# Quarter 3's down-projections as pairs of 128x64 matrices, with a new written-out instruction order

## The chip, the cores and the metric

One core of a Trainium2 chip runs the whole program. The metric is the time of one execution on the device, in microseconds (us), as the median of several runs; lower is better. Engines are named as in the profile: PE is TensorE (PEld its weight loads), DVE is VectorE, ACT is ScalarE, POOL is GpSimd, SP is the queue that issues most DMAs.

## What is computed

```python
def _A_ref(q, k, v, shift_k, ssm_k, ssm_D):      # B=1, S=2048, D=512
    # k_shift[t] = sum over 4 taps of k[t - j] * shift_k[:, j]
    kv = k_shift * v
    # y = causal long convolution of kv with ssm_k along S, by FFTs of length 2S
    y = y + kv * ssm_D[None, None, :]
    return q * y

def _B_ref(x, w_gate, w_up, w_down):             # 512 -> 1792 -> 512
    h = _gelu(x @ w_gate) * (x @ w_up)
    return h @ w_down

x = A_q
xn = _layernorm(x, axis=-1)
s = _A_ref(xn, A_k, A_v, A_shift_k, A_ssm_k, A_ssm_D)
g = _silu(_B_ref(xn, B_w_gate, B_w_up, B_w_down))
return x + s * g
```

All inputs are bf16.

## The kernel before

The 2048 rows are cut into four quarters of 512. The feed-forward part does, for each quarter `q` (0 to 3), fourteen units: a unit is one 128-column block of the gate and of the up projection, four matmuls of 128x128 weights against 512 columns of the transposed normalised input `xnT` for each of the two. ACT takes the gelu of the gate out of PSUM (`GE`, line 1194), DVE multiplies it with the up product (`HT`, line 1203), which also gives the PSUM bank back. `down(q)` then multiplies `HT` with `Wd`: per 128-row tile `jt` fourteen 128x128 matmuls of 512 columns that add up in one PSUM bank, in three tasks of 4, 5 and 5. For the last tile of quarter 3 the columns are split 384 + 128, so that the very last piece is short. `xnT` of quarters 0 and 1 is made on PE; that of quarters 2 and 3 by one DMA transpose each (line 884), issued from SP, in a single buffer per quarter parity. The normalisation of a tile (`XN`, lines 870 on ACT and 871 on DVE) may be placed on either engine.

The convolution part is a staged transform. Its PE work is in smaller matrices: halves of 64x128 (lines 950 and 959), 32x32 matrices, sixteen side by side (line 1028, for `BH`, `BK` and the inverse `MI`), and, as its last stage (line 1270, called y below), eight pieces j of two pairs each: two 128x64 matrices side by side, one writing PSUM partitions 0 to 63, the other 64 to 127, at `tile_position=(0, 0)` and `(0, 64)`. Between the stages the data passes through DRAM scratch (`ZH`, `ZK`, `ZI`) and comes back transposed by DMA into `BH`, `BK`, `BI`. The 32x32 stage on `BH` is evicted to `HSW` by ACT or DVE, a swap of its rows by two DMAs (`HSW<-HSW`) makes a second copy, and DVE multiplies these with the evicted `KB` (line 1131).

For y, a piece is copied out of PSUM (`BO`, line 633 on ACT or 636 on DVE) and multiplied by DVE into `G` or `XN` (line 1287), for tiles 0 to 11 with the residual added (line 1299) and sent out. For quarter 3, ACT takes the Silu of the down-projection (line 1235), and DVE multiplies and adds (lines 1237 and 1238) before the output DMA.

The order is written out by hand-off: `SEQ` is a list of 816 task numbers (a `b` behind a number takes the task's second engine, DVE in place of ACT or the reverse), found by a search; every engine gets its instructions in that order, and semaphores hold each until its inputs are there. At most four PSUM banks (`NF_BANKS = 4`) belong to units and down-projections at a time. `SEQ`, the costs and due times beside it say what the search assumed; at run time only the order counts.

Of the kernel before, what the change touches and what calls it, by code (L numbers as in the profile page):

```python
# [7 lines left out]
FP32 = mybir.dt.float32  # L8
# [10 lines left out]
MF = FF // 128  # L19
NQ = 4  # L20
# [4 lines left out]
N_WARM = 12  # L25
ORDER = "x00 h0 x01 w0 D0 h1 w1 h2 h3 s0 k0 w2 x1 k1 k2 w3 d0 d1 v0 v1 k3 v2 v3 x2 x3"
SEQ = (
# [23 lines left out]
)  # L51
NF_BANKS = 4
ISSUE = 470.0
# [361 lines left out]
def build_kernel(nc, A_q, A_k, A_v, A_shift_k, A_ssm_k, A_ssm_D, B_w_gate, B_w_up, B_w_down, out):  # L415
    with ExitStack() as es0:
# [11 lines left out]
        def new(name, shape, dt):  # L428
            h = at(name, shape, dt, place["at"])
            place["at"] += size(shape, dt)  # L430
            return h
# [3 lines left out]
        Wd = new("Wd", [128, MF, DM], BF16)  # L435
# [10 lines left out]
        ident = new("ident", [128, 128], BF16)  # L446
        ident32 = new("ident32", [128, 128], FP32)
        COLS = new("COLS", [128, 8], FP32)
        stats = new("stats", [128, NT, 6], FP32)
        mv = new("mv", [128, NT, 4], FP32)  # L450
        NHALF = new("NHALF", [128, 4, 1], FP32)
        EPSC = new("EPSC", [128, 1, 1], FP32)
        NB_ = new("NB_", [128, NT, 1], FP32)
        SKB = new("SKB", [128, 4, DM], BF16)
        skb_at = place["at"] - 4 * DM * 2
# [9 lines left out]
        HT = new("HT", [128, 2, MF, 512], BF16)  # L465
# [51 lines left out]
        trk = Trk(nc, block)  # L517
# [15 lines left out]
        def R_bank(b):  # L533
            return [R_ps[b.slot // 2][b.slot % 2]]
# [19 lines left out]
        R_HT = [[res(f"HT{j}_{m}", HT[:, j, m, :]) for m in range(MF)] for j in range(2)]  # L554
# [86 lines left out]
        def mm(h, o, l, r, st, sp):  # L641
            return h.matmul(o, lhsT=l, rhs=r, start=st, stop=sp)  # L642
# [145 lines left out]
        R_Wd = [res(f"Wd{i}", Wd[:, 7 * i:7 * i + 7, :]) for i in range(2)]  # L788
# [137 lines left out]
        for k in range(KD):  # L926
# [4 lines left out]
                    r=[bHD, *[bHTr[k][0] for k in range(KD)]], w=[bFold], rr=[R_D, *R_HTr[0]], ww=R_HTr[0])  # L931
# [274 lines left out]
        def down(q):  # L1206
            for jt in range(4):
                t = 4 * q + jt
                cols = [(0, DM)] if t < NT - 1 else [(0, 384), (384, DM)]
                for c0, c1 in cols:  # L1210
                    p = B(f"psd{q}_{jt}_{c0}", pF)

                    def pc(p=p, c0=c0, c1=c1):
                        return bank(p)[:, c0:c1]

                    for m0, m1 in ((0, 4), (4, 9), (9, 14)):
                        def f(e, p=p, jt=jt, m0=m0, m1=m1, pc=pc, c0=c0, c1=c1):
                            for m in range(m0, m1):
                                trk.op("PE", lambda h, m=m: mm(h, pc(), HT[:, q % 2, m, 128 * jt:128 * (jt + 1)], Wd[:, m, c0:c1], m == 0, m == MF - 1),
                                       r=[R_HT[q % 2][m], R_Wd[m // 7]], w=R_bank(p), accum=True)  # L1220
                        down_tasks[q].append(S.add([("PE", pe(m1 - m0, c1 - c0))], f, r=(bHT[q] if jt else bHT[q][m0:m1]) + bWd[m0 // 7:(m1 + 6) // 7],
                                                   w=[p], lat=150.0))
                    n = c1 - c0
                    g, rg = G[:, t, c0:c1], [R_G[t] if n == DM else R_Gh[c0 > 0]]
                    bt = B(f"tanh{q}_{jt}")
                    if q < NQ - 1:
# [3 lines left out]
                           r=[p, bt], w=[bG[t // 2]], rr=lambda p=p, rg=rg: R_bank(p) + rg, ww=rg)  # L1230
# [11 lines left out]
                          r=[b2], w=[B(f"outl{t}")], nbytes=256 * n)  # L1242
# [14 lines left out]
        for j in range(8):  # L1257
            p, bi = p_y[j], b_bi[j]
# [98 lines left out]
```

## Time and profile before

| | |
|---|---|
| median of 3 runs | 190.72 us (190.45 to 190.84) |
| span of the profiled execution (first to last instruction) | 189.2 us |
| granted TensorE clock, mean | 0.997 |
| PE busy | 182.8 us, 1406 matmuls recorded |
| DVE busy | 165.5 us, 250 instructions |
| ACT busy | 141.6 us, 196 instructions |

The profile has no time of its own for that execution beside its span: the 1.5 us between 189.2 and 190.72 lie around the span (start and end of the program). Busy time of PE overlaps from one matmul to the next: a matmul's row lasts about 0.38 us though one starts every 0.216 us, so the distance between starts is what counts. Some matmul records are missing, 1406 of 1418; where one is missing the profile shows 0.16 us of "issue" on PE or a row with one matmul fewer.

### The profile page before, as it was taken

The numbers are of one execution on the slowest core, as the hardware profiler recorded it, in microseconds if no ns is written. First come the engines' busy times: TensorE is split into PE (matmuls) and PEld (weight loads), VectorE is DVE, ScalarE is ACT, GpSimd is POOL, SyncE is SP. The second block draws the span as 40 slices with busy tenths as digits, with TensorE's granted clock in tenths as the row PEclk, the third lists the DMA queues.
The fourth block names the chain that finished last, engine by engine and source line by source line (L and its number), as shares of the span: only waits on it lengthen the run. The fifth ranks groups of instructions, "written<-read, shape, count | busy, mean of one in ns | idle before, by whom it ended". The sixth has DMA issues, their size and how long they took to land.

```text
span 189.2 us, 3591 instructions
## 1 busy us (share of the span) xinstructions
PE 182.8 (97%) x1406; PEld 80.6 (43%) x1418; DVE 165.5 (87%) x250; ACT 141.6 (75%) x196; POOL 10.4 (5%) x26
## 2 busy tenths in 40 slices
PE   7899999999999999999999999999999999999992
PEld 2685544544333334334444443433333344444441
DVE  6889999999999999978589599999999964658695
ACT  3749797998879798799638897998999575323971
POOL 5312302000000000022000000000000000000000
PEclk9999999999999999999999999999999999999998
DMA  5999999999584996557999997499345254908754
GB/s 177 319 381 297 366 380 360 402 415 297 166 309 150 335 287 229 166 187 235 301 310 173 333 322 251 144 299 326 135 162 170 97 181 146 376 36 283 268 186 153
DMA packets 36422, 47.84 MB, mean 253 GB/s; under 512 B 7347, under 2 KB 26039, under 8 KB 36406
## 3 DMA queue, kind: packets, MB, share of 16 engines
q1 hardware_dynamic: 29878, 39.23, 63.6%
q10 hardware_dynamic: 6528, 8.39, 12.8%
q8 instruction: 11, 0.18, 0.4%
q14 instruction: 5, 0.04, 0.1%
HBM read 27.39 MB, written 14.68 MB: 222 GB/s over the span
## 4 chain that ended last, share of the span: by engine, by line
PE 79%; DVE 15%; ACT 3%; issue 2%
PE psall L642 67%; PE psall L1028 6%; DVE KTM L1009 3%; DVE KAC L1011 2%; PE psall L916 2%; PE psall L950 2%; DVE HT L1203 1%; DVE G L1299 1%; PE psall L959 1%; PE psall L1270 1%; DVE G L1287 1%; DVE XN L965 1%; DVE G L1238 1%; DVE G L1237 1%; ACT XN L870 1%
## 5 line engine op out<-in xcount | busy, mean ns | idle before, releaser
L642 PE MATMUL psall<-xnT,Wu 128*128 128x512 bf16 (+1 forms) x248 | 56.0, 359 | 0.0
L642 PE MATMUL psall<-xnT,Wg 128*128 128x512 bf16 (+1 forms) x248 | 55.3, 359 | 0.5 <-DVE xnT L636 0.5
L642 PE MATMUL psall<-Wd,HT 128*128 128x512 bf16 (+2 forms) x226 | 50.3, 366 | 1.2 <-issue 0.8
L1194 ACT ACTIVATE GE<-psall 128x512 bf16<-128x512 f32 x54 | 31.7, 605 | 10.5 <-PE psall L642 10.0
L1203 DVE TENSOR_TENSOR HT<-psall,GE 128x512 bf16<-128x512 f32 x43 | 29.1, 685 | 8.0 <-PE psall L642 7.8
L642 PEld LDWEIGHTS psall<-xnT,Wu 128*128 128x128 bf16 x248 | 22.5, 98 | 26.0 <-issue 2.3
L642 PEld LDWEIGHTS psall<-xnT,Wg 128*128 128x128 bf16 x248 | 21.7, 98 | 26.7 <-issue 2.3
L642 PEld LDWEIGHTS psall<-Wd,HT 128*128 128x128 bf16 x238 | 21.4, 98 | 27.4 <-issue 5.4
L633 ACT ACTIVATE BO<-psall 128x1024 bf16<-128x1024 f32 x22 | 22.0, 1024 | 9.6 <-PE psall L1270 5.8
L1131 DVE TENSOR_TENSOR HSW<-KB,HSW 128x2048 bf16<-128x2048 bf16 x16 | 19.2, 1217 | 0.0
L633 ACT ACTIVATE HSW<-psall 128x1024 bf16<-128x1024 f32 x16 | 15.5, 1036 | 2.3 <-PE psall L1028 2.2
L633 ACT ACTIVATE KB<-psall 128x1024 bf16<-128x1024 f32 x14 | 13.8, 1028 | 2.6 <-PE psall L1028 2.4
L1011 DVE TENSOR_TENSOR KAC<-KAC,KTM 128x2048 bf16<-128x2048 bf16 x12 | 14.6, 1216 | 0.1
L1009 DVE TENSOR_TENSOR KTM<-KK,SKB 128x2048 bf16<-128x2048 bf16 x12 | 14.6, 1214 | 0.1
L633 ACT ACTIVATE AST<-psall 128x1024 bf16<-128x1024 f32 x12 | 12.3, 1023 | 1.9 <-PE psall L950 1.5
L1227 ACT ACTIVATE G<-psall 128x512 bf16<-128x512 f32 x12 | 7.2, 597 | 5.7 <-PE psall L642 4.5
L849 DVE BATCH_NORM_STATS2 stats<-X 128x6 f32<-128x512 bf16 x16 | 10.6, 672 | 0.5 <-DMA X<-in_A_q_dram 0.5
L1229 DVE SCALAR_TENSOR_TENSOR G<-G,psall 128x512 bf16<-128x512 bf16 x12 | 8.1, 680 | 3.0 <-ACT G L1227 3.0
L1131 DVE TENSOR_TENSOR KB<-KB,HSW 128x2048 bf16<-128x2048 bf16 x8 | 9.6, 1220 | 0.1
L1154 DVE TENSOR_TENSOR HSW<-HSW 128x2048 bf16<-128x2048 bf16 x8 | 9.5, 1217 | 0.0
L862 POOL TENSOR_TENSOR mv<-mv,NHALF 128x1 f32<-128x1 f32 (+1 forms) x7 | 5.3, 754 | 70.7 <-DVE mv L860 66.1
L633 ACT ACTIVATE X<-psall 128x1024 bf16<-128x1024 f32 x8 | 8.1, 1018 | 1.1 <-PE psall L959 1.0
(88 smaller groups left out, 163.4 us busy)
## 6 DMA issues: line engine op xcount, KB each, us to landing
BH<-ZH SPq DMA_DIRECT2D x8, 512.0 KB, 5.9
BK<-ZK SPq DMA_DIRECT2D x8, 512.0 KB, 5.8
HSW<-HSW SPq DMA_DIRECT2D x16, 256.0 KB, 3.1
ZI<-BO ACTq DMA_DIRECT2D x16, 256.0 KB, 2.9
BI<-ZI SPq DMA_DIRECT2D x8, 512.0 KB, 5.0
ZK<-AST SPq DMA_DIRECT2D x6, 512.0 KB, 3.4
Hn<-in_A_ssm_k_dram SPq DMA_DIRECT2D x4, 512.0 KB, 7.5
KK<-in_A_k_dram SPq DMA_DIRECT2D x4, 512.0 KB, 10.7
```

The costliest lines, as they stand in the source:

```text
L633: return h.activation(o, i, ACTF.Copy, scale=scale)
L642: return h.matmul(o, lhsT=l, rhs=r, start=st, stop=sp)
L849: t_stats[t] = op([("DVE", 670.0)], lambda e, h, t=t: h.bn_stats(stats[:, t, :], X[:, t, :]), r=[bX[q][t % 4]], w=[bst[t]], rr=[R_X[t]], w ...
L1009: op([("DVE", dur)], lambda e, h, j=j, m=m: h.tensor_tensor(KTM[:, m.slot, :, :], kk(j), sk(j), ALU.mult), r=need + [bSKB[j], a], w=[m], r ...
L1011: op([("DVE", dur)], lambda e, h, m=m: h.tensor_tensor(KAC[:, a.slot, :, :], KAC[:, a.slot, :, :], KTM[:, m.slot, :, :], ALU.add), r=[m], ...
L1028: trk.op("PE", lambda h: h.matmul(ps(s, i)[b, :], lhsT=wt(col)[a, :], rhs=data(col)[a, :], start=n < 16, stop=n >= len(todo) - 16, tile_po ...
L1131: return hd.tensor_tensor(pair(KB, *(2 * DM * z for z in slots())) if to else x, k, x, ALU.mult)
L1154: return hd.tensor_tensor(x, x, y, ALU.add)
L1194: op([("ACT", act(512))], lambda e, h: h.activation(GE[:, g.slot, :], bank(pg), ACTF.Gelu_apprx_tanh), r=[pg], w=[g], rr=lambda: R_bank(pg ...
L1203: op([("DVE", dve(512, 1))], lambda e, h: h.tensor_tensor(HT[:, q % 2, m, :], bank(pu), GE[:, g.slot, :], ALU.mult), r=[pu, g], w=[bHT[q][m]],
L1227: op([("ACT", act(n))], lambda e, h, g=g, pc=pc: h.activation(g, pc(), ACTF.Tanh, scale=0.5), r=[p], w=[bt], rr=lambda p=p: R_bank(p), ww= ...
L1229: op([("DVE", dve(512, 1))], lambda e, h, g=g, pc=pc: h.scalar_tensor_tensor(out=g, in0=g, scalar=1.0, in1=pc(), op0=ALU.add, op1=ALU.mult ...
```

## The change

Two things are changed, and one without effect on work (the constants `NHALF` and `EPSC` stand at another SBUF address).

First, in `down(3)` every matmul of more than 128 columns becomes two, one for each half of the 128 rows of the tile: weights of 128x64, the same moving data `Wd`, outputs in partitions 0 to 63 and 64 to 127 of the same bank. That is the form of the y stage. The last piece of 128 columns stays as it was. PE gets 56 more matmuls and as many more weight loads.

Second, `SEQ` is another list. The loads at the start, on SP, stand in the same order, the first PE groups too; behind them much is moved by a place or a few, on every engine.

```diff
 SEQ = (
-    "0 2 3 16 1 17 18 10 4 6 48 19 20 5 21 7 22 23 8 9 24 25 26 11 49 27 28 29 67 68 76b 30 31 32 65 66 73 12 77 78 74 75 69 87 91 86 90b 365 366 70 "
...
+    "2 0 3 4 7 10 8 11 16 67 9 5 12 68 65 17 76b 66 6 1 77 18 48 73 74 49 19 78 50 75 87 86 69 90b 365 91 70 377 378 79b 366 71 20 379 369 21 72 82 367 80 "
...
 )
@@
-        NHALF = new("NHALF", [128, 4, 1], FP32)
-        EPSC = new("EPSC", [128, 1, 1], FP32)
@@ down(q)
                     for m0, m1 in ((0, 4), (4, 9), (9, 14)):
-                        def f(e, p=p, jt=jt, m0=m0, m1=m1, pc=pc, c0=c0, c1=c1):
+                        paired = q == NQ - 1 and c1 - c0 > 128
+
+                        def f(e, p=p, jt=jt, m0=m0, m1=m1, pc=pc, c0=c0, c1=c1, paired=paired):
                             for m in range(m0, m1):
+                                if paired:
+                                    for i in range(2):
+                                        c = slice(64 * i, 64 * i + 64)
+                                        trk.op("PE", lambda h, m=m, i=i, c=c: h.matmul(pc()[c, :], lhsT=HT[:, q % 2, m, 128 * jt + 64 * i:128 * jt + 64 * i + 64], rhs=Wd[:, m, c0:c1], start=m == 0, stop=m == MF - 1, tile_position=(0, 64 * i)),
+                                               r=[R_HT[q % 2][m], R_Wd[m // 7]], w=R_bank(p), accum=True)
+                                    continue
                                 trk.op("PE", lambda h, m=m: mm(h, pc(), HT[:, q % 2, m, 128 * jt:128 * (jt + 1)], Wd[:, m, c0:c1], m == 0, m == MF - 1),
                                        r=[R_HT[q % 2][m], R_Wd[m // 7]], w=R_bank(p), accum=True)
```

How PE's instructions stand at the end, as counts of matmuls (y is line 1270; "down" is quarter 3's down-projection, 512, 384 or 128 columns):

```
before: units ..., y 12, down 18, y 8, down 4 (384) + 10, y 8, down 9, y 4, down 5 + 10 (384), down 14 (128)
after:  units ..., y 8, pairs 8, y 4, pairs 8 (384) + 18, y 4, pairs 10, y 4, pairs 10, y 4,
        pairs 18, y 4, pairs 10, y 4, pairs 10 + 20 (384), down 14 (128)
```

("pairs 8" is eight 128x64 matmuls, four pairs.)

Three places further up that the prediction speaks of. The four `XN` normalisations of quarter 3 feed its DMA transpose on SP; the numbers of PE instructions (604) and of changes between matrix sizes (36) ahead of the first gate matmul of quarter 3 are the same in both orders.

```
ACT before: ... HSW x4, XN, G (tanh), HSW x2, KB, XN ...
ACT after:  ... HSW x3, G (tanh), HSW x2, XN (the last of quarter 3), XN (quarter 2), KB ...
SP  before: BK, BK, HSW swap, xnT transpose (quarter 3), HSW swap, BH, BK, xnT transpose (quarter 2), ...
SP  after:  BK, BK, HSW swap, BH, xnT transpose (quarter 3), HSW swap, BK, xnT transpose (quarter 2), ...
DVE before: ... HSW x2 (line 1131), G x2, KB product, HT, KB product, HSW product, HT x2 ...
DVE after:  ... HSW (line 1131), G x2, KB product x2, HSW product, HT x2 ...
```

In the list of before, the last normalisation of quarter 3 to finish is on DVE (line 871). Ahead of the last `ZK` store, ACT of before has the two evictions that fill its buffer back to back; after the change one gelu stands between the two. On ACT at the end, before has two `BO` evictions, two more, the table load for Silu, two Silus and three `BO`; after has five `BO`, the load, one Silu, two `BO`. Four PSUM evictions in all go from ACT to DVE (DVE 250 to 254 instructions).

More of the change, by code (lines that the diff above doesn't have):

```diff
@@ L448, in build_kernel @@
         COLS = new("COLS", [128, 8], FP32)
+        NHALF = new("NHALF", [128, 4, 1], FP32)
+        EPSC = new("EPSC", [128, 1, 1], FP32)
         stats = new("stats", [128, NT, 6], FP32)
         mv = new("mv", [128, NT, 4], FP32)
-        NHALF = new("NHALF", [128, 4, 1], FP32)
-        EPSC = new("EPSC", [128, 1, 1], FP32)
         NB_ = new("NB_", [128, NT, 1], FP32)
@@ L1221, in down @@
                         down_tasks[q].append(S.add([("PE", pe(m1 - m0, c1 - c0))], f, r=(bHT[q] if jt else bHT[q][m0:m1]) + bWd[m0 // 7:(m1 + 6) // 7],
-                                                   w=[p], lat=150.0))
+                                                   w=[p], lat=150.0, mode=3 if paired else 0))
                     n = c1 - c0
```

43 rows, old and new, of the table SEQ are left out of this document.

## The prediction

> **What bounds the kernel now.** I read the page's busy times and its chain first: which engine has no room.
>
> ```profile
> span 189.2 us, 3591 instructions
> ...
> PE 182.8 (97%) x1406; PEld 80.6 (43%) x1418; DVE 165.5 (87%) x250; ACT 141.6 (75%) x196; POOL 10.4 (5%) x26
> ...
> PE 79%; DVE 15%; ACT 3%; issue 2%
> ```
>
> PE carries 79% of the chain, and the 97% are nearly all there is, since the rest is the start and the last microseconds. So a stall of PE anywhere after the start, and every piece of PE time saved, moves the end one for one, as long as the last microseconds follow. The second reading is therefore PE's timeline at the end, where the change is, third the other engines there, fourth the inputs that arrive by DMA, because an order that was found anew can be late only where something that isn't PE's arrives late.
>
> ```profile
> 159.60 1.03 PE L642 MATMUL psall<-xnT,Wu 128*128 128x512 bf16 x4
> 160.47 1.03 PE L642 MATMUL psall<-xnT,Wg 128*128 128x512 bf16 x4
> ...
> 174.60 1.05 PE L1270 MATMUL psall<-BI,G 128*64 128x512 bf16 x8
> 175.59 2.98 PE L642 MATMUL psall<-Wd,HT 128*128 128x384 bf16 x14
> ...
> 181.53 0.62 PE L1270 MATMUL psall<-BI,G 128*64 128x512 bf16 x4
> 182.09 3.66 PE L642 MATMUL psall<-Wd,HT 128*128 128x512 bf16 x29
> ```
>
> Starts are what to read (start, length, engine). From 159.60 to 160.47 four full matmuls: 0.87 / 4 = 0.217 us each. From 174.60 to 175.59 a visit of y with four pairs takes 0.99, from 181.53 to 182.09 one with two pairs 0.56: two pairs more cost 0.43, so a pair of 128x64 matrices costs 0.215, the same as one full matmul.
>
> **Part 1, the pairs.** A full matmul of `down(3)` becomes a pair: 42 of 512 columns and 14 of 384, at 0.215 against 0.217, which I count as nothing: 56 more matmuls and loads lie inside the slots, as they do in y. What covers the loads is the running pair. Here a rule speaks against the change.
>
> ```profile
> L642 PEld LDWEIGHTS psall<-Wd,HT 128*128 128x128 bf16 x238 | 21.4, 98 | 27.4 <-issue 5.4 <-ACT G L1227 0.2
> ...
> L1270 PEld LDWEIGHTS psall<-BI,G 128*64 128x64 bf16 x32 | 1.5, 109 | 2.5 <-issue 1.3 <-DVE HT L1203 0.4
> ```
>
> A load of 64 columns takes 109 ns, one of 128 takes 98. But 32 loads of 109 ns sum to 3.5 us and occupy 1.5: the two of a pair run over each other. (The Trainium skill, "TensorEngine Tiling (Array Packing)", Restrictions, says that column tiling disables Fast Weight Load; the 109 beside 98 agrees that half the columns aren't loaded in less time. It is a rival below.)
>
> What is saved is the change between matrix sizes.
>
> ```profile
> 181.22 0.38 PE L642 MATMUL psall<-Wd,HT 128*128 128x512 bf16 x1
> ```
>
> From 181.22 to 181.53 one full matmul took 0.31, 0.094 over its 0.217: the way in. The visit of two pairs took 0.56, 0.13 over 0.43: the first pair and the way out. A visit so costs 0.22 us beyond its work. Before, the end has four visits; after, y and the down pairs are one stretch, with one way in and one way out (ahead of the last 128-column piece). Three visits fall away: **-0.67 us** on PE.
>
> **Part 2, the last microseconds.**
>
> ```profile
> 177.07 0.69 DVE L1299 TENSOR_TENSOR G<-G,X 128x1024 bf16<-128x1024 bf16 x1
> 179.17 0.43 DVE L1237 TENSOR_TENSOR G<-G,XN 128x512 bf16<-128x512 bf16 x1 [1.41 <-ACT G L1235]
> ...
> 186.69 0.22 DVE L1237 TENSOR_TENSOR G<-G,XN 128x128 bf16<-128x128 bf16 x1
> 186.94 0.22 DVE L1238 TENSOR_TENSOR G<-G,X 128x128 bf16<-128x128 bf16 x1
> ```
>
> ```profile
> 177.25 1.28 ACT L1235 ACT_TABLE_LOAD   x1
> ...
> 185.78 0.28 ACT L1235 ACTIVATE G<-psall 128x128 bf16<-128x128 f32 x1 [0.29 <-PE psall L642]
> ```
>
> ```profile
> out_dram<-G SPq DMA_DIRECT2D x1, 32.0 KB, 1.6
> ```
>
> DVE lost 1.41 us at 179.17 waiting for the first Silu, which stood behind a table load of 1.28. It never got this back: the last Silu ended at 186.06, and with 0.22 + 0.22 behind it DVE could have ended at 186.50, but ended at 187.16, 0.66 late. The last output lands 1.6 after that, fixed. After the change the y pieces are spread over seven visits, five `BO` evictions in place of four stand ahead of the table load, so DVE has y products to do during it, and only three large y operations follow its first Silu product instead of seven. The backlog shrinks: between 0 and -0.66. Silus and evictions still come close together on ACT at the end, so I take a little under half, **-0.30**. Four evictions that go from ACT to DVE add work to DVE that is inside this.
>
> **Part 3, the order above.** The start (same loads, same first PE groups) I count at nothing; what covers it is that the first loads and PE's first groups follow each other as before. If it were otherwise, by one small thing, some 0.2 either way. The place that matters is around 88 to 106 us.
>
> ```profile
> 88.57 4.88 SPq L884 DMA_TRANSPOSE xnT<-XN  x1
> 93.49 1.22 SPq L615 DMA_DIRECT2D HSW<-HSW  x2
> ...
> 96.15 5.04 SPq L884 DMA_TRANSPOSE xnT<-XN  x1
> ```
>
> ```profile
> DMA to landing us min/median/max: 6.6/6.8/7.0
> ```
>
> ```profile
> 87.62 0.71 DVE L871 TENSOR_SCALAR XN<-X,mv 128x512 bf16<-128x512 bf16 x2
> ```
>
> ```profile
> 87.35 0.82 ACT L870 ACTIVATE XN<-X,NB__69,mv 128x512 bf16<-128x512 bf16 x1
> ...
> 89.02 1.94 ACT L633 ACTIVATE HSW<-psall 128x1024 bf16<-128x1024 f32 x2 [0.37 <-PE psall L1028]
> ```
>
> ```profile
> 97.99 1.03 PE L642 MATMUL psall<-xnT,Wg 128*128 128x512 bf16 x4
> ```
>
> The four normalisations of quarter 3 end on DVE at 87.62 + 0.71 = 88.33, the transpose is issued 0.24 later at 88.57, occupies SP for 4.88 and lands 6.6 after its issue (the other 7.0): 95.2. The first gate matmul that reads it starts at 97.99; the margin is 2.8 us. After the change the last of the four is on ACT behind the pair of `HSW` evictions, which wait for PE and can't end before 89.02 + 1.94 = 90.96. Then 0.82 for the normalisation and 0.24: issue at 92.0, landing between 98.6 and 99.0. The same 604 PE instructions stand ahead of the gate matmul, which is due at 97.99 again. PE waits 0.6 to 1.0: **+0.80**. Behind PE's wait everything is queued, PE runs in order.
>
> The transpose holds SP until 92.0 + 4.9 = 96.9, so the next `HSW` swap is issued at 97.0 and 97.6 instead of 93.49.
>
> ```profile
> HSW<-HSW SPq DMA_DIRECT2D x2, 256.0 KB, 3.5
> ```
>
> ```profile
> 99.43 1.22 DVE L1131 TENSOR_TENSOR KB<-KB,HSW 128x2048 bf16<-128x2048 bf16 x1
> 100.56 0.68 DVE L1203 TENSOR_TENSOR HT<-psall,GE 128x512 bf16<-128x512 f32 x1
> 101.16 1.22 DVE L1131 TENSOR_TENSOR KB<-KB,HSW 128x2048 bf16<-128x2048 bf16 x1
> ```
>
> It landed 3.5 us after issue, the mean of its two (the row is for this swap alone). Then both halves are there at about 101, and DVE's `KB` product that started at 99.43 starts 1 to 1.5 us later. Worse, the new order puts the first `HT` product of quarter 3, which gives back a PSUM bank, behind two `KB` products and an `HSW` product (1.13 from start to start) rather than one: 101 + 3 x 1.13 = 104.4 against 100.56. That product ends 0.7 later, at 105.1, the next one 0.6 behind it. From its late start at 98.8 PE has 28 matmuls and two 32x32 stages (0.217 and a visit's 0.22 each) ahead of the next gate matmuls, 28 x 0.217 + 0.87 = 7.0, so it asks for banks again from 105.8 on. With both halves of the swap at 101 the first bank is just free, the second just so; each 0.1 later is 0.1 of wait, and a late DVE hands its delay on to the releases behind. The swap's two halves need not land together: if one is a microsecond late, PE waits 0.3 for the first bank and up to 0.9 more for those behind. Bounds 0 and 1.2; the mean landing is at the edge, so I take the middle, **+0.60**. The quarter-2 transpose behind it is issued at about 98.9, lands at 105.5 to 105.9, and its first reader is due at
>
> ```profile
> 105.83 0.39 PE L642 MATMUL psall<-xnT,Wg 128*128 128x512 bf16 x1
> ```
>
> four matmuls earlier in the new order but behind the 0.80: no further wait.
>
> Sum: -0.67 - 0.30 + 0.80 + 0.60 = +0.43. The span goes from 189.2 to 189.6; with the 1.5 around it, from the median of 190.72 to **191.15 us**. About 0.2% (0.38 us) is what a measurement of this kernel can tell from no change.
>
> **The rivals.** *Only the gate matmul waits* (the swap is early, the bank free in time): -0.67 - 0.30 + 0.80 = -0.17, 190.55. For it: the bank's margin is not in any row; against it: SP's queue is full there. Chance 0.18.
>
> *Nothing waits.* The transpose's 4.88 on SP would have to be mostly competition with the transfers beside it, or ACT's evictions earlier: -0.97, 189.75, faster. Against it: the other transpose took 5.04 with other neighbours. Chance 0.17.
>
> *PE waits already for `BH`*, 10 us earlier.
>
> ```profile
> 81.39 0.36 SPq L615 DMA_DIRECT2D ZK<-AST  x1
> 83.32 0.36 SPq L615 DMA_DIRECT2D BH<-ZH  x1
> ```
>
> ```profile
> BH<-ZH SPq DMA_DIRECT2D x1, 512.0 KB, 4.3
> ```
>
> ```profile
> 88.47 0.43 PE L1028 MATMUL psall<-BH,TF 32*32 32x512 bf16 x16
> ```
>
> The load lands at 83.32 + 4.3 = 87.6, 0.85 ahead of its matmuls. The `ZK` store ahead of it is now behind one gelu more on ACT and so 0.5 to 0.85 later. If the load is late by more than the 0.85, the wait comes on top, and the evictions and the transpose behind it move along; with a stall as large again as that margin, 191.15 + 0.85 = 192.0; beyond that point every 0.1 decides. Slower; chance 0.13.
>
> *The 64-column loads are not covered* when the weights are new for each pair: 2 x 109 = 218 ns in a slot of 215, and of 161 for 384 columns (three quarters of 215): 42 x 3 + 14 x 57 = 0.92 us on top, 192.1. Against it: y's loads run over each other. Chance 0.05. (This is what the Trainium skill's restriction above would do.)
>
> *The pairs don't run side by side* while they add up in one bank: 42 x 0.215 + 14 x 0.161 = 11.3, about 202. The change would not be what it says. Against it: y's pairs write one bank too. Chance 0.02.
>
> **How the numbers follow.** The forecast, waits at the gate matmul and behind it, has 0.45; its own range is 190.8 to 191.9 (0.35 less with the gate's wait at 0.6 and the bank's at 0.4, 0.8 more with 1.0 and 1.2). Some 0.12 of it falls inside 0.2%, 0.33 above. *Only the gate* is centred inside, with 0.05 of its 0.18 below 190.34. So faster 0.17 + 0.05 = 0.22; same 0.12 + 0.13 = 0.25; slower 0.33 + 0.13 + 0.05 + 0.02 = 0.53. The range reaches from nearly the clean case, 189.9, to just over the two rivals above, 192.4; the serial pairs and the lowest part of the clean case are left out.
>
> **What would show it.** In the profile after: PE's end in one stretch of 128x64 with starts 0.215 apart; one way in, one way out; DVE with no wait for the Silu, ending less than 0.66 behind what the last Silu allows; the quarter-3 transpose issued at 92 rather than 88.57; PE idle for 0.6 to 1.0 before the first gate matmul of quarter 3, put down to a DMA, and idle again for `HT` (line 1202, before 1203) between 103 and 109. It is wrong if the gate matmul starts at 98 without idle time, if pairs start more than 0.22 apart, or if PE's idle time lies elsewhere, at the y stage's `BI` loads above all.

## The result, and the profile after

The changed kernel takes 192.52 us (median of six runs, 191.35 to 193.85), the kernel before 190.68 beside it: a ratio of 1.0098, 95% interval 1.0069 to 1.0128. Slower was right, 191.15 was not: 192.52 lies just over the end of the range, and the loss is four times the one forecast. The runs after also scatter over 2.5 us, those of before over 0.6. Two later runs (194.68 us in `taps_in_order`, 193.29 in `bk_swap_bh`) took over 1.5% more than the fastest of their kernel and are left out of its time and ratio.

Line numbers of the new kernel are one lower than before up to the down-projection; the paired matmul is line 1223, y 1277, the Silu product 1244, the last sum 1245. First the page (busy times, then the chain that ended last, by engine and by line).

```profile
span 191.0 us, 3695 instructions
...
PE 182.5 (96%) x1463; PEld 81.4 (43%) x1474; DVE 170.6 (89%) x254; ACT 137.8 (72%) x192; POOL 15.0 (8%) x26
...
PE 76%; DMA 9%; ACT 6%; DVE 6%; issue 2%; ACTq 0%
PE psall L641 59%; PE psall L1027 5%; PE psall L1223 4%; DMA xnT<-XN 4%; DMA BK<-ZK 4%; PE psall L958 2%; PE psall L915 2%; PE psall L949 2%; PE psall L1277 2%; ACT XN L869 1%; DMA ZK<-ASX 1%; ACT GE L1193 1%; ACT AST L632 1%; DVE HT L1202 1%; ACT ASX L632 1%
```

PE's busy time hardly moved, and the chain now contains 9% DMA, 4% each on the quarter-3 transpose and on `BK`. Before, the chain's line names no DMA. Next, PE's timeline, three rows with idle time in brackets:

```profile
30.32 0.61 PE L958 MATMUL psall<-HTr,F 64*128 64x512 bf16 x4 [0.91 <-DVE HT L1202]
...
93.19 0.44 PE L1027 MATMUL psall<-BK,TF 32*32 32x512 bf16 x16 [0.46 <-DMA BK<-ZK]
...
100.64 1.89 PE L641 MATMUL psall<-xnT,Wg 128*128 128x512 bf16 x8 [1.03 <-DMA xnT<-XN]
```

The same PE instruction starts 0.0 us later than before up to about 25 us, 0.92 later at 85, 1.45 at 96, 2.64 from 109 to 162, and the last weight load starts at 187.43 instead of 185.47, 1.96 later. So there are three losses in this execution, at 30, 93 and 100 us, and one gain, at the end:

```profile
173.58 0.60 PE L1277 MATMUL psall<-BI,G 128*64 128x512 bf16 x4
174.02 2.76 PE L1223 MATMUL psall<-Wd,HT 128*64 128x384 bf16 x26
176.61 0.60 PE L1277 MATMUL psall<-BI,G 128*64 128x512 bf16 x4
177.04 1.25 PE L1223 MATMUL psall<-Wd,HT 128*64 128x512 bf16 x10
```

Two pairs of y take 174.02 - 173.58 = 0.44, with pairs of down on either side: 0.22 a pair and nothing for the visit, where a visit of two pairs before cost 0.56. And the queue on SP, with the transposed load:

```profile
85.94 0.91 SPq L614 DMA_DIRECT2D BK<-ZK  x2
86.89 1.72 SPq L614 DMA_DIRECT2D HSW<-HSW  x2
88.66 0.86 SPq L614 DMA_DIRECT2D BH<-ZH  x1
92.64 4.28 SPq L883 DMA_TRANSPOSE xnT<-XN  x1
96.97 1.23 SPq L614 DMA_DIRECT2D HSW<-HSW  x2
```

```profile
BK<-ZK SPq DMA_DIRECT2D x2, 512.0 KB, 7.6
```

The two `BK` loads took 7.6 us to land (mean); before it was 4.6. The transpose landed 7.9 us after its issue. Each load is carried by sixteen queue engines with a completion each in the trace: those of the first `BK` load ended 4.0 us apart, at 89.0 to 93.05; before, 0.6 us apart. The transpose waits for the last of them, and for the `BH` load in between.

### The profile page after: what moved, and what is told of

Its sections match the earlier page's. It is cut to its first block, busy times and chain, and to the rows that moved or that the text cites. A ratio compares the mean times of both kernels' runs of the same rounds, so it can differ in the third digit from the quotient of the medians.

```text
span 191.0 us, 3695 instructions
## 1 busy us (share of the span) xinstructions
PE 182.5 (96%) x1463; PEld 81.4 (43%) x1474; DVE 170.6 (89%) x254; ACT 137.8 (72%) x192; POOL 15.0 (8%) x26
## 4 chain that ended last, share of the span: by engine, by line
PE 76%; DMA 9%; ACT 6%; DVE 6%; issue 2%; ACTq 0%
PE psall L641 59%; PE psall L1027 5%; PE psall L1223 4%; DMA xnT<-XN 4%; DMA BK<-ZK 4%; PE psall L958 2%; PE psall L915 2%; PE psall L949 2%; PE psall L1277 2%; ACT XN L869 1%; DMA ZK<-ASX 1%; ACT GE L1193 1%; ACT AST L632 1%; DVE HT L1202 1%; ACT ASX L632 1%
## 5 line engine op out<-in xcount | busy, mean ns | idle before, releaser
L641 PE MATMUL psall<-Wd,HT 128*128 128x512 bf16 (+1 forms) x171 | 39.0, 367 | 1.1 <-issue 0.3
L641 PEld LDWEIGHTS psall<-xnT,Wu 128*128 128x128 bf16 x248 | 22.0, 98 | 26.3 <-issue 2.3
L632 ACT ACTIVATE BO<-psall 128x1024 bf16<-128x1024 f32 x20 | 19.9, 1022 | 9.7 <-PE psall L1027 4.9
L641 PEld LDWEIGHTS psall<-Wd,HT 128*128 128x128 bf16 x182 | 16.2, 98 | 21.0 <-issue 2.6
L632 ACT ACTIVATE HSW<-psall 128x1024 bf16<-128x1024 f32 x15 | 14.8, 1025 | 3.2 <-PE psall L1027 3.1
L632 ACT ACTIVATE KB<-psall 128x1024 bf16<-128x1024 f32 x12 | 12.1, 1026 | 4.0 <-PE psall L1027 3.6
L1223 PE MATMUL psall<-Wd,HT 128*64 128x512 bf16 (+1 forms) x112 | 12.5, 366 | 0.0
L861 POOL TENSOR_TENSOR mv<-mv,NHALF 128x1 f32<-128x1 f32 (+1 forms) x7 | 6.3, 903 | 66.4 <-DVE mv L859 61.8
L632 ACT ACTIVATE AST<-psall 128x1024 bf16<-128x1024 f32 x10 | 10.3, 1033 | 0.2
L632 ACT ACTIVATE XN<-psall 128x1024 bf16<-128x1024 f32 x7 | 7.2, 1031 | 2.8 <-PE psall L958 2.7
```

The costliest lines, as they stand in the source:

```text
L632: return h.activation(o, i, ACTF.Copy, scale=scale)
L1223: trk.op("PE", lambda h, m=m, i=i, c=c: h.matmul(pc()[c, :], lhsT=HT[:, q % 2, m, 128 * jt + 64 * i:128 * jt + 64 * i + 64], rhs=Wd[:, m, ...
```

## The experiments

Theory after these readings: the pairs are worth what was forecast, the new order loses three times as much, at the start through the tap copies on POOL and at 93 and 100 us through SP's queue. Rival: the paired form itself costs. Ratios are to the kernel before, run on the same chip; intervals are 95%.

### The two parts alone

`pairs_old_order` keeps the `SEQ` of before and takes the pairs; `new_order_no_pairs` is the other half:

```diff
-                        paired = q == NQ - 1 and c1 - c0 > 128
+                        paired = False
```

> The pairs alone, in the instruction order of before: y and quarter 3's down-projections become one stretch of 128x64 matrices. Theory (the pairs gain, the new order loses): three visits of 0.22 us fall away on PE, no new wait; DVE at the end stays late behind the table load, so the end gains between 0.2 and 0.67: 190.0 to 190.5 us, PE's last matmul 0.6 to 0.7 earlier than before. Rival (the pairs themselves cost, by their weight loads): slower than before, by 0.5 to 0.9 us, with starts of pairs over 0.22 apart.

> The new order with full matmuls, no pairs: y now stands in seven visits among 128x128 matmuls. Theory (the order loses, the pairs gain): the waits of the changed kernel stay, and the end has seven visits instead of one, 6 x 0.22 = 1.3 us more: 193.4 to 194.2 us. Rival (the pairs cost): as fast as the changed kernel or faster, 191.5 to 192.5.

Pairs in the old order: 190.51 us, ratio 0.9979 (0.9961 to 0.9996), no idle time of 0.2 us or more on PE after the start. New order without pairs: 193.63, ratio 1.0135 (1.0105 to 1.0166), with the waits for `BK` and the transpose on PE as in the changed kernel:

```profile
92.79 0.44 PE L1027 MATMUL psall<-BK,TF 32*32 32x512 bf16 x16 [0.46 <-DMA BK<-ZK]
100.27 1.89 PE L641 MATMUL psall<-xnT,Wg 128*128 128x512 bf16 x8 [1.06 <-DMA xnT<-XN]
```

On PE the pairs save in both orders: from the last unit to the last weight load PE gains 0.68 us in `pairs_old_order`, as in the changed kernel, and loses 0.68 in `new_order_no_pairs`. By time alone this is clear of noise in the old order only; in the new one the two intervals (up to 1.0128, from 1.0105) overlap. The order loses 1.4%, and the rival, that the pairs cost, is out.

In the old order little of PE's gain reaches the end. This is the last sum of `pairs_old_order`:

```profile
186.23 0.22 DVE L1245 TENSOR_TENSOR G<-G,X 128x128 bf16<-128x128 bf16 x1
```

Its last Silu ends at 184.90, so DVE ends at 186.46, 1.12 us behind what the Silu allows, against 0.66 before: PE has become 0.68 earlier since the last unit, the end only 0.23. With the new tail DVE is 0.47 behind, in the changed kernel as in `t90` below.

### The step on the transpose

`norm_on_dve` writes the last normalisation of quarter 3 on DVE, early, as before, so that the transpose can be issued earlier (`b` takes the second engine):

```diff
-... 670 673 671 577 194 672b 262 ...
+... 670 673 671 672 577 194 262 ...
```

> The changed kernel, with quarter 3's last normalisation back on DVE behind the three others, where DVE then stands idle: the transpose is issued as soon as SP has issued the BH load ahead of it, near 90.5 us instead of 92.6. Theory (the gate matmul waits for a transpose that is issued late): its wait of 1.03 us goes, the time falls by 0.8 to 1.1, to 191.4 to 191.8. Rival (another wait stands right behind it, for the swap's rows or a PSUM bank): the idle time comes back by 109 us and the time falls by less than 0.3.

193.12 us, ratio 1.0103 (1.0078 to 1.0127): nothing gained. SP's row and the first gate matmuls:

```profile
90.24 7.25 SPq L883 DMA_TRANSPOSE xnT<-XN  x1
```

```profile
101.14 1.89 PE L641 MATMUL psall<-xnT,Wg 128*128 128x512 bf16 x8 [1.07 <-DMA xnT<-XN]
```

Issued 2.4 us earlier, it held SP 3.0 us longer, landed 10.8 us after its issue instead of 7.9, and the wait stayed. The issue was not what made it late. `bh_behind` takes the `BH` load (196) out of its way, and `bh_behind_norm_dve` does both:

```diff
-... 190 553 196 264b 563 674 550 ...
+... 190 553 264b 563 674 196 550 ...
```

> The changed kernel, with the second load into BH issued behind quarter 3's xnT transpose on SP, as in the kernel before, instead of ahead of it. Theory (the transpose's landing is set by the transfers queued ahead of it on SP): without the 512 KB of that load the two BK loads take 5 to 6 us instead of 7.6, the 0.46 us wait for BK goes, the transpose issued at 92.6 lands 6.5 to 7 us later instead of 7.9, and TensorE's wait ahead of the gate matmul falls from 1.03 to 0 to 0.4: about 191.5 us, 1 us under the changed kernel. Rival (the queue is slow there for another reason, the store of ZK or the swaps): BK 7 us or more, transpose 7.5 to 8, time 192.3 to 192.7.

> The changed kernel with both edits: the second BH load behind the transpose, and the normalised tile of quarter 3 written by VectorE ahead of the swap's products, as in the kernel before. Theory (queue ahead plus issue): transpose issued at about 90, landing at 96.5 to 98, no wait of TensorE between 88 and 101, 191.0 to 191.4 us, what is left over the kernel before being the 0.9 us lost in the first 30 us less the 0.7 that the pairs save. Rival (the issue itself is slow with the loads in flight, as with the norm alone on VectorE): SP takes 7 us for it, landing past 100, time 192.5 or more.

191.87 (1.0051, 1.0034 to 1.0068) and 192.18 (1.0075, 1.0056 to 1.0094). In `bh_behind`:

```profile
92.30 3.27 SPq L883 DMA_TRANSPOSE xnT<-XN  x1
```

```profile
DMA to landing us min/median/max: 5.3/5.3/5.3
```

```profile
BK<-ZK SPq DMA_DIRECT2D x2, 512.0 KB, 7.9
```

Issued as late as in the changed kernel, the transpose lands after 5.3 us, and the gate matmul's wait is gone: the theory on what stands ahead of it held. But `BK` is as slow as ever, 7.9, so the `BH` load behind it was not its cause (PE idles 0.71 ahead of the `BK` matmul); there the rival was right. With `BH` out of the way, the earlier norm adds nothing: issued at 91.00, the transpose landed after 7.3 us, no wait followed at the gate matmul, and the 191.0 to 191.4 us expected were missed.

### The start

`taps_in_order` lets POOL copy the taps in the order 3, 2, 1, 0 again (one number, 143, moved up). `extra_copies` is the kernel before with eight more copies on POOL that nobody reads, beside DVE's products:

```diff
+            for n in range(8):
+                trk.op(e, lambda h: h.tensor_copy(SCR[:], SKB[:, 3, :]), r=[R_SKB[3]], w=[R_SCR])
```

> The changed kernel, with one of POOL's four copies of the convolution taps moved: the one that DVE's first multiply (line 1008) needs is copied second, as before the change, and not last. Theory (PE's wait of 0.91 us at 30 us comes from DVE, which stood 0.54 us for POOL's last copy): DVE's wait goes, PE's wait at 30 falls to 0.3 to 0.5, the time falls by 0.4 to 0.6, to 191.9 to 192.1. Rival (DVE is late there by its own order and by slower instructions beside POOL's copies): PE still waits 0.8 or more, time within 0.2 of the changed kernel.

> The kernel before with eight more GpSimd copies of 128x512 (a tap to a scratch tile that nobody reads) right behind the four tap copies, beside VectorE's products of 128x2048 from two SBUF tiles. Theory (GpSimd's and VectorE's SBUF-to-SBUF work take turns, which is why the four tap copies of the changed kernel took 6.0 us instead of 2.4): the eight take 1.0 to 2 us each, 8 to 14 us in all, and VectorE's products or sums beside them grow from 1.2 to 1.3 us to 1.5 us and more, or wait between; TensorE then waits for HT at 30 us, and the time rises by 0.5 to 2 us. Rival (the tap copies were long for another reason, the DMAs at the start): 0.65 us each, VectorE unchanged, 190.7 us.

The rows of the four tap copies before and after, and the DVE product that waits for them in the changed kernel:

```profile
17.92 2.42 POOL L986 COPY SKB<-SKR 128x512 bf16<-128x512 bf16 x4 [7.58 <-DMA SKR<-in_A_shift_k_dram]
```

```profile
18.23 6.00 POOL L985 COPY SKB<-SKR 128x512 bf16<-128x512 bf16 x4 [7.99 <-DMA SKR<-in_A_shift_k_dram]
```

```profile
24.27 1.23 DVE L1008 TENSOR_TENSOR KTM<-KK,SKB 128x2048 bf16<-128x2048 bf16 x1 [0.54 <-POOL SKB L985]
```

`KTM` lies where the raw taps lay, so its first product waits for all four copies. They end 3.9 us later than before, DVE loses 0.54, its `HT` product comes late, and PE waits 0.91 at 30 us. `taps_in_order` took 192.07 (1.0063, 1.0039 to 1.0087): copies 4.4 us in all, PE's wait 0.27. That the product needs tap 2 alone, as I had it, was wrong.

Nor can the 0.27 be put down to the order of the taps. Eight other kernels here have the start of the changed kernel untouched, and their traces fall into two groups:

| traces | four copies | begin behind DVE's two `HTr` copies | PE's wait for `HT` | PE late at 85 us |
|---|---|---|---|---|
| changed kernel, `norm_on_dve`, `bh_behind`, `bh_behind_norm_dve`, `bk_reads_zh` | 6.0 to 6.1 | 1.75 to 2.3 | 0.89 to 0.91 | 0.6 to 1.75 |
| `new_order_no_pairs`, `bk_behind_swap`, `bk_swap_bh`, `bk_waits` | 3.5 to 4.1 | 0.8 to 1.5 | 0.24 to 0.30 | 0.3 to 0.5 (`bk_swap_bh` 2.7, see below) |

(The third column counts from the start of the first of the two, 16.41 in the changed kernel.) So the new start has two values with one and the same order. What separates the groups is the moment at which the copies begin, which is when their load has landed (a difference between traces, not one that a run set); `taps_in_order`, at 1.2 us, would stand in the second group without its edit and shows nothing on the taps. Of the traces with the start of before, none but `extra_copies` (below) has a wait of PE for `HT` there. What makes the copies long is their neighbours on DVE. `extra_copies` shows this in the order of before (191.46, ratio 1.0039, 1.0024 to 1.0054), groups on POOL:

```profile
L993 POOL COPY SCR<-SKB 128x512 bf16<-128x512 bf16 x8 | 9.6, 1199 | 0.4
...
L987 POOL COPY SKB<-SKR 128x512 bf16<-128x512 bf16 x4 | 2.4, 650 | 7.7 <-DMA SKR<-in_A_shift_k_dram 7.7
```

and DVE beside them:

```profile
24.05 1.21 DVE L1018 TENSOR_TENSOR KTM<-KK,SKB 128x2048 bf16<-128x2048 bf16 x1
25.29 1.52 DVE L1020 TENSOR_TENSOR KAC<-KAC,KTM 128x2048 bf16<-128x2048 bf16 x1
```

The four tap copies take 650 ns each beside DVE's work that is mostly out of PSUM. The 1199 ns are a mean of two kinds: the first four extra copies, beside DVE's sums and products of two SBUF tiles, took 1.09, 1.75, 2.81 and 1.49 us, the last four, beside DVE's work out of PSUM or on one tile, 0.62 each. Of DVE's operations one is longer (1.52 for 1.2). In the changed kernel's trace DVE has the 128x1024 sums and the first `KAC` product during the tap copies (18.7 to 24.2 us), and one of these sums took 1.02 us for 0.67 to 0.70; before, they stand behind the copies. (The Trainium skill, "SBUF — State Buffer", section "SBUF: two separate sides", says that GpSimd and VectorE operations with two SBUF inputs take turns at one pair of ports, whole instructions at a time. The trace agrees with the turns; that the one which comes second simply waits fits POOL here, DVE hardly ever.)

### Where in the order the loss arises

Four kernels with the pairs take the order of before up to a moment and the new one from there (tasks that started before that moment in the profile of before stand as there): `cut31`, `cut60`, `cut70`, `cut84`; `t90` takes only the last 90 of the 816 tasks, from the middle of the final stretch, in the new order.

> The paired form with the order before for all but the last 90 tasks, which keep the new order (the pairs with the tail they were planned with). Theory (the loss lies in the new order of the first 105 us, and the new tail itself does no harm): no wait of TensorE after the start, 189.8 to 190.4 us, at or under the old order with pairs (190.51). Rival (the new tail costs something too): 190.8 or more.

> The paired form in the order of the kernel before for all work that started there before 31 us, and in the new order for the rest. Theory (the loss has two places, 0.9 us in the first 31 us and about 1.5 us between 88 and 101 us): no wait of TensorE for HT at 30 us, four tap copies on GpSimd under 4.5 us, the waits for BK (0.3 to 0.7) and xnT (0.8 to 1.1) as in the changed kernel: 191.4 to 191.8 us. Rival (the late start is made good by slack later): no change, 192.3 or more.

> The paired form in the order before up to 60 us, the new order from there. The first BK load's sixteen queue engines end 2.2 to 4.0 us apart in every kernel with the new order, 0.6 to 1.1 us apart with the old one. If what comes from 60 us on makes that: spread over 2 us, waits for BK and xnT at 93 and 100 us, 191.4 to 191.8 us. If it comes from ahead of 60 us: spread under 1.2 us and 190.0 to 190.8 us.

> The same with the border at 70 us: the loads of X and BH at 66 to 74 us as in the kernel before, the stores of ZK from 75 us on in the new order. Theory (the stores from 75 us on and what VectorE and ScalarE do beside them set it): spread over 2 us, 191.4 to 191.8. Rival (the earlier loads): spread under 1.2 us, 190.0 to 190.8.

> The same with the border at 84 us, right ahead of the two BK loads: the queue comes to them as in the kernel before, but quarter 3's normalisation is still written by ScalarE and the second BH load still goes ahead of the xnT transpose. Theory (the transpose is late because of its queue as well as its issue): BK spread under 1.2 us and no wait for it, transpose issued at 90.5 to 92 and landing 6 to 7 us later, wait ahead of the gate matmul 0 to 0.6: 190.0 to 190.7 us. Rival (the late issue alone makes the wait, as the prediction had it): 0.6 to 1.0 us of wait, 190.8 to 191.4.

| | time | ratio (interval) | wait at the `BK` matmul | wait at the gate matmul | spread of `BK`'s engines |
|---|---|---|---|---|---|
| changed kernel | 192.52 | 1.0098 (1.0069 to 1.0128) | 0.46 | 1.03 | 4.0 |
| `cut31` | 192.95 | 1.0124 (1.0084 to 1.0164) | 1.10 | 1.05 | 4.3 |
| `cut60` | 192.24 | 1.0073 (1.0052 to 1.0094) | 1.55 | 1.00 | 4.4 |
| `cut70` | 192.72 | 1.0095 (1.0068 to 1.0122) | 0.79 | 1.00 | 3.8 |
| `cut84` | 190.90 | 1.0005 (0.9993 to 1.0018) | 0 | 0 | 1.2 |
| `t90` | 189.72 | 0.9944 (0.9928 to 0.9960) | 0 | 0 | 1.1 |

`cut31`, `cut60` and `cut70` missed their times. In `cut60`, with no stall at 30 us, PE comes to the `BK` matmul earlier and waits there longer (1.55 for 0.46). The trace of `cut31` is of a run of 194.92, and PE waits 1.55 for ACT at 49.6 us in it. The seam of the two orders need not be the cause: `bk_swap_bh` has no seam, and in its trace, of the run of 193.29, PE waits 1.69 for ACT at the same matmul. The border lies between 70 and 84 us. `cut84` is the telling one:

```profile
92.21 1.97 SPq L883 DMA_TRANSPOSE xnT<-XN  x1
```

```profile
DMA to landing us min/median/max: 4.3/4.3/4.3
```

```profile
85.83 3.20 PE L641 MATMUL psall<-Wd,HT 128*128 128x512 bf16 x14 [1.08 <-DVE HT L1202]
...
98.48 1.89 PE L641 MATMUL psall<-xnT,Wg 128*128 128x512 bf16 x8
```

The norm is on ACT, the issue as late as forecast (92.21), the `BH` load still ahead, and yet the transpose lands after 4.3 us, at 96.5, and the gate matmul at 98.48 has no wait. (The 1.08 at 85.83 is a seam of the two orders and makes most of what this kernel takes more than `t90`.) So the late issue alone costs nothing; `t90` shows that the new tail is sound, and is faster than the kernel before, the changed one and the pairs in the old order (190.51).

### What makes BK slow

`bk_behind_swap` issues the swap (190) ahead of the two `BK` loads (261, 274), `bk_swap_bh` also moves 196 behind the transpose, `cut60_bk_swap_bh` does both with the old order up to 60 us:

```diff
-... 668 669 261 548 ... 263 274 190 553 ...
+... 668 669 190 261 548 ... 263 274 553 ...
```

> The changed kernel with the two-transfer swap of the 84 to 87 us stretch issued ahead of the two BK loads instead of behind them. In the new order the BK loads start 0.0 to 0.2 us after the last ZK store has landed, in the old one 2 us after fifteen of its sixteen queue engines have. Theory (rows read from memory that soon after they were written are slow on some of the engines): BK issued 1.3 to 2 us later, its engines end at most 1.5 us apart instead of 4.0, it lands at 92 to 93 although issued later, the second BH load and the transpose behind it land up to 1.5 us earlier, the wait ahead of the gate matmul falls from 1.0 to under 0.4, 191.3 to 191.9 us. Rival (the spread has another cause): still 3 us and more, BK and transpose later by the 1.3 us, TensorE waits 1.5 us or more for BK, 193 us or more.

> The same, and the second BH load behind the transpose as well. Theory: transpose landing 5.5 to 6.5 us after its issue, no wait for BK nor for xnT, 191.0 to 191.5, 0.3 to 0.8 us over the old order with pairs less what the first 31 us cost. Rival (the BK loads are slow for another reason): a wait for BK of 1.5 us or more, 192.3 or more.

> The paired form with the old order up to 60 us, the new order from there, and both edits of the SP queue. Theory (start, BK and BH ahead of the transpose are all that the new order loses): no wait of TensorE of more than 0.3 us, 189.8 to 190.5 us, at the old order with pairs (190.51) and under the kernel before. Rival: a wait for BK of 1.5 us and 191.5 to 192.3 us, as without the edits.

191.28 (1.0030, 1.0009 to 1.0052), 190.75 (1.0001, 0.9985 to 1.0016) and 190.28 (0.9978, 0.9965 to 0.9990). SP and the loads in `bk_behind_swap`:

```profile
86.98 1.10 SPq L614 DMA_DIRECT2D BK<-ZK  x2
88.13 0.57 SPq L614 DMA_DIRECT2D BH<-ZH  x1
92.04 2.02 SPq L883 DMA_TRANSPOSE xnT<-XN  x1
```

```profile
BK<-ZK SPq DMA_DIRECT2D x2, 512.0 KB, 4.5
```

Issued 1.04 us later, `BK` lands 4.5 us after issue instead of 7.6, so at 91.05 and 92.51 instead of 93.05 and 94.41; its engines end 0.8 us apart; the transpose lands after 4.3; and PE waits for neither. This one exchange on the queue takes 1.2 us off. With `BH` moved too and the order of before up to 60 us, the kernel is under the one before: 190.28. That isn't all of the loss: `t90`, with the same tail, is at 0.9944 against 0.9978. In the two traces this difference arises ahead of 15 us (PE is 0.68 us ahead of the kernel before in `t90`, 0.07 behind it here), in the order of before; its cause stays open.

Whether the freshly stored rows of `ZK` are slow to read, or the moment of issue counts, was asked of two more: `bk_reads_zh` reads rows that were stored long before, at the old moment; `bk_waits` lets the first `BK` load wait for an ACT eviction at the same place in the queue.

```diff
-z_rows(ZK, 4 * n, 4), d_bk[bk.slot], R_Z["K"],
+z_rows(ZH if n in (0, 4) else ZK, 4 * n, 4), d_bk[bk.slot], R_Z["K"] + R_Z["H"],
```

```diff
-d_bk[bk.slot], R_Z["K"],
+d_bk[bk.slot], R_Z["K"] + ([R_HS[bHS[0].slot][0]] if n == 0 else []),
```

> The changed kernel in its own order, but the two BK loads of the 86 us stretch read the same rows of ZH, which were stored long before, in place of ZK (so two frequency groups of the convolution are computed from other data; the waits, the sizes and the layout stay). Theory (memory rows are slow to read right after they were stored): issued at 85.9 as before, engines at most 1.5 us apart, BK landing by 91.5, the transpose by 97.5 to 98.5, wait ahead of the gate matmul under 0.4, 191.0 to 191.7 us. Rival (the queue or the moment of issue makes the spread): 3 to 4 us apart, waits and time as in the changed kernel, 192.2 to 193.

> The changed kernel in its own order of instructions, but the first BK load also waits for the ScalarE eviction that ends at 87.5 us, so both BK loads go 1.5 us later with nothing put between the store and them; the swap goes 1.5 us later too. Theory (time since the store): issued at 87.5, engines at most 1.5 us apart, landing at 91.5 and 93 or earlier than the 93.05 and 94.41 of the changed kernel, 191.2 to 192.0 us. Rival (it was the swap put in between that helped): still 3 us apart, landing at 94.5 or later, 193 us or more.

192.51 (1.0066, 1.0040 to 1.0093) and 191.27 (1.0037, 1.0018 to 1.0057). The loads of the one, then of the other:

```profile
BK<-ZH SPq DMA_DIRECT2D x2, 512.0 KB, 7.0
```

```profile
BK<-ZK SPq DMA_DIRECT2D x2, 512.0 KB, 4.9
```

Old rows are read slowly too (7.0, engines 2.8 apart) when the load goes at the old moment: so my theory of fresh rows fell. `bk_waits`, where the load goes 1.6 us after the last store has landed rather than at once, is fast (4.9, engines 1.3 apart); that would fit the theory as well, but it rules out the rival, since no swap stands in between. (Its gate matmul still waits 0.45, with the `BH` load ahead.) What the profiles divide by is the time since the `BH` load ahead: 1.7 to 2.2 us in the kernels whose `BK` engines end 2.2 to 4.4 apart, 2.7 to 3.4 in those where they end 0.6 to 1.3 apart. (The time since the last `ZK` store divides them too, 2.8 to 3.4 against 4.4 to 5.1.) Which of the two it is, and why some of the sixteen engines then fall microseconds behind, stays open.

## Why the prediction was wrong

Three steps failed: the start, put at nothing; the `BK` load, for which there was no term; and the landing of the transpose, taken as its issue plus 6.6 to 7.0 us. A fourth, the bank wait, was counted and did not come. The column on the right is of the profiled executions.

| step | predicted | measured |
|---|---|---|
| Part 1, three visits fewer, pairs as one matmul | -0.67 | -0.68 (PE's lag 2.64 to 1.96) |
| Part 2, the last microseconds | -0.30 | -0.19 (DVE's end +1.77 against PE's +1.96) |
| Part 3, the start | 0, 0.2 either way | +0.92 |
| `BK` at 93 us | no term | +0.53 (lag 0.92 to 1.45), 0.46 of it in the row |
| wait ahead of the gate matmul | +0.80 | +1.19 (lag 1.45 to 2.64), 1.03 of it in the row |
| swap, `HT`, PSUM bank | +0.60 | 0 |
| sum | +0.43 | +1.77, the span's 189.2 to 191.0 |

**Parts 1 and 2** stand. (In the prediction's range, 0.2 less at the gate and 0.2 less at the bank make 0.40, not 0.35, a small slip.) The 26 matmuls from 174.02 to 176.61 are four pairs of 384 columns and nine of 512: 4 x 0.161 + 9 x 0.215 = 2.58 by the prediction, 2.59 measured. The rivals on loads and on pairs that don't run side by side are out. The backlog behind Silu's load shrank as argued, by less:

```profile
183.28 0.42 DVE L1244 TENSOR_TENSOR G<-G,XN 128x512 bf16<-128x512 bf16 x1
184.18 0.69 DVE L1294 TENSOR_TENSOR G<-BO,G 128x1024 bf16<-128x1024 bf16 x1 [0.48 <-ACT BO L632]
...
188.70 0.23 DVE L1245 TENSOR_TENSOR G<-G,X 128x128 bf16<-128x128 bf16 x1
```

The first Silu product has no wait, but DVE then waited 0.48 for a `BO`, and still ended 0.47 behind what the last Silu (188.02) allows, against 0.66 before. That this part depends on the tail's order, and without it eats most of Part 1, is what `pairs_old_order` adds.

**The start** is the largest miss. That "the first loads and PE's first groups follow each other as before" is true and covers nothing: the order of DVE beside POOL changed, and with it PE waits for `HT` at 30 us in all ten traces that have the new start. The step looked at PE and SP, and never at POOL. The size is that of one execution: where the copies were shorter, PE was 0.3 to 0.5 late at 85 us. How much of the 0.92 reaches the end depends on what waits later: `cut60` and the changed kernel differ by 0.28, within their scatter, because the wait for `BK` took it over; with the queue mended the order of before up to 60 us is worth 190.75 - 190.28 = 0.47.

**The gate matmul's wait** came, at the place and from the transfer forecast, at 1.03, but the step that led to it failed, that the landing is the issue plus 6.6 to 7.0. The issue came at 92.64 (92.0 forecast), and with that issue the landing took 8 us in the changed kernel, 5.3 without the `BH` load ahead, and 4.3 behind a queue that was not held up. The 6.6 of before was mostly a wait itself: by the completions, the swap ahead landed at 93.3, 4.8 us after the transpose's issue, and the transpose 1.8 behind it. The other transpose, which the prediction held against its rival *Nothing waits* since it took as long with other neighbours, had a queue ahead as well: it landed 1.75 behind the `BK` load ahead of it (101.36). In `cut84` quarter 3's transpose landed at 96.5, 2 us ahead of its reader, where the forecast had a loss of 0.8 with the same issue. That 1.03 lies near 0.80 is luck: PE came to the gate matmul 1.45 late, so a landing 6.6 to 7.0 behind the issue, at 99.2 to 99.6, would have left it a wait of 0.2 at most. And PE's idle time at 30 and 93 us is what the prediction had named as a sign of being wrong.

**The rival on `BH`** did not come true: that load landed at 87.94, and its matmul started at 89.38 without a wait. **The bank wait** did not come either. SP let the swap go at 96.97, as forecast (97.0), and DVE did wait for it:

```profile
101.70 2.36 DVE L1130 TENSOR_TENSOR KB<-KB,HSW 128x2048 bf16<-128x2048 bf16 x2 [0.34 <-DMA HSW<-HSW]
...
106.48 1.29 DVE L1202 TENSOR_TENSOR HT<-psall,GE 128x512 bf16<-128x512 f32 x2 [1.16 <-PE psall L641]
```

But the `HT` product then waited 1.16 for PE: PE was 2.64 late by then, not 0.80, and asked for the bank that much later. Two waits in a row were added up where the first, being larger, had already paid for the second.

## What to carry to other kernels

A DMA's time from issue to landing, read in one profile, holds for the queue as it stood there: before moving an issue, subtract what was queued ahead of it, and look at the moments of the loads in front too. When an order is found anew, compare every pair of engines that share something, POOL and DVE at the start of this one, not only the engine that bounds. And test the two halves of a change apart: here a sound edit (0.2% in the order of before, 0.6% with the new tail as well) came with an order that lost 1.4%. Last, look at the same stretch in several traces before giving an edit the credit: the start had two values with nothing changed.

## What was not expected of the hardware

Sixteen engines of one load can end 4 us apart, and what stands behind it in the queue landed late as well: issuing the load 1 us later made it land 2 us earlier. Among transposes of the same 512 rows, SP was held between 1.97 and 7.25 us and the landing took 4.3 to 10.8. A GpSimd copy of 128x512 took 0.62 to 0.66 us beside DVE's work out of PSUM or on one SBUF tile, 1.1 to 2.8 beside its sums and products of two SBUF tiles, and 1.5 on average in the changed kernel. A visit of y among full matmuls, from one matrix size to the other and back, cost PE 0.22 us, and three visits fewer gave 0.68, which is the whole gain of the pairs on PE.
